# Regrouping the first two chunks of a windowed-attention and feed-forward kernel: tile 0 of the four batches, with exps divided before their transpose

## The chip, the cores and the metric

The kernel runs on one NeuronCore of a Trainium2 chip. The metric is the device time of one execution in microseconds (us). The engines are PE (TensorE, matmuls), DVE (VectorE), ACT (ScalarE), POOL (GpSimd) and SP (SyncE, which issues the DMAs here).

## What is computed

```python
# q, k, v: (4 batches, 8 heads, 768 positions, 64), n_sink = 4, window = 128
scores = q @ k^T / sqrt(64)
keep = (key position < n_sink) | (0 <= row - key < window)
a = softmax(where(keep, scores, -1e9))
x = (a @ v) as (4 * 768 tokens, 512)
h = x @ w_in                      # 512 x 2048
g = where(h > 0, h, exp(min(h, 0)) - 1)
out = g @ w_out                   # 2048 x 512
```

All is float32 to the outside; the weights arrive as 64-bit words.

## The kernel before

Tokens are cut into 24 tiles of 128 (6 for each of the 4 batches, NT = 6), and tiles into chunks. `SIZES` (L42) gives nine chunks of consecutive tiles, 2, 2, 2 and then six of 3. A tile attends to its own and the previous tile of its batch, and to the four sink keys. So tile 0 of a batch has one key block of 4 + 128 columns (KW = 132), every other tile has two (264 columns), and tiles 2 to 5 have the sinks as a separate part. Heads go in four pairs.

For each chunk, attention yields x for four head pairs, each as two float16 parts, high and low. Then the feed-forward runs 16 steps of f (`feed_forward`, L881): 12 matmuls h <- x, w (L902), the exponential unit on ACT and DVE (L910, L912, L915), a split into two float16 parts (L916 on ACT, L918 on DVE in chunk 0 and L921 on POOL elsewhere), and then, two steps later, three matmuls for each tile into accumulators (L932). Chunks 0 and 1 go in halves, (0, first 8 f), (1, first 8 f), (0, last 8 f), (1, last 8 f), because the weights are still arriving: `weights(k)` (L474) loads 32 pieces of 512 KB, rebuilds each value from its 64-bit word (d on ACT L339, sign on DVE L343 or POOL L340, bits on DVE L344, POOL L341 or ACT L342, v on DVE L345) and splits it into two float16 parts (L502 on ACT, L503 on POOL).

There are two attentions. `attention_f32` (L559) serves chunks 0 and 1 (`TURNED`, L50), all in float32: scores (L600), a reduction with the mask (L607, DVE), exps with their sums (L610, ACT), transposes of the exps on PE (L617), their copy out of PSUM (L621), the sums' scaling on POOL (L622) and the reciprocal (L623), sink columns (L628, L643, L646), then values (L658, L663), and a matmul that spreads 1/sum over the partitions (L666). The result is multiplied by 1/sum behind the values: the spread 1/sum goes to SBUF (rx, L679, ACT), DVE multiplies (L680), and the product is split (L682 on ACT, L683 on DVE or POOL). One PSUM bank, `po`, serves all of this in turn. `attention` (L690) serves the other chunks: from chunk 3 on (`WHOLE`) keys and queries are split into float16 parts (L717, L720, L721), scores are two matmuls per head (L791, L792), probabilities are split into two float16 parts (L827, L828), transposed by DMA, and multiplied with both parts of v (L861; sinks L866). Chunk 2 takes its scores in float32 (L797) and the rest as chunks 3 on.

The order of the work comes from a planner (`Plan`, L99): each piece is a task with an engine or a choice of engines, a cost and its dependencies. PE's tasks have hand-given positions (`times`, L518: a slot is half a feed-forward step), the others take due times from their users. Rings (`RINGS`, L53) limit buffers. The masks of tile 1 and of the tiles behind are tasks of their own (L457, L458), as are the limits (L459). In the first 28 us warm-up matmuls (L1273) fill PE's planned pauses. Checks of the value range (L987, L994, L1009) run on DVE with no user but the end.

## Time and profile before

| | |
|---|---|
| time, median of 3 runs | 615.57 us (615.26 to 615.84) |
| time of the profiled execution | 615.47 us |
| its span, first to last instruction | 613.7 us |
| PE busy | 603.9 us (98%), 4608 matmuls |
| DVE busy | 480.3 us (78%) |
| ACT busy | 435.1 us (71%) |
| POOL busy | 263.5 us (43%) |
| granted TensorE clock, mean | 0.998 |

A busy share is an average over stages. In the profile's 40 slices DVE and ACT are at 8 to 9 tenths in the first seven and PE at 9 in all but the first and the last. Line numbers (L902) are those of the kernel before.

### The profile page before, as it was taken

The numbers are of one execution on the slowest core, as the hardware profiler recorded it, in microseconds if no ns is written. First come the engines' busy times: TensorE is split into PE (matmuls) and PEld (weight loads), VectorE is DVE, ScalarE is ACT, GpSimd is POOL, SyncE is SP. The second block draws the span as 40 slices with busy tenths as digits, with TensorE's granted clock in tenths as the row PEclk, the third lists the DMA queues.
The fourth block names the chain that finished last, engine by engine and source line by source line (L and its number), as shares of the span: only waits on it lengthen the run. The fifth ranks groups of instructions, "written<-read, shape, count | busy, mean of one in ns | idle before, by whom it ended". The sixth has DMA issues, their size and how long they took to land.

```text
span 613.7 us, 13669 instructions
## 1 busy us (share of the span) xinstructions
PE 603.9 (98%) x4608; PEld 365.2 (60%) x4608; DVE 480.3 (78%) x1284; ACT 435.1 (71%) x1236; POOL 263.5 (43%) x510
## 2 busy tenths in 40 slices
PE   9899999999999999999999999999999999999996
PEld 6666665677775565655555565655555565555553
DVE  8999989979989877797788988887897987533232
ACT  6999999878888776677677767666876866332222
POOL 3878777543344433333344444223434444222211
PEclk9999999999999999999999999999999999999999
DMA  8776975959789775483867857585756935310001
GB/s 308 266 263 219 239 258 193 232 114 230 193 155 218 160 151 128 105 222 95 180 146 185 210 112 157 129 222 137 199 124 158 232 69 136 98 45 9 2 0 58
DMA packets 117360, 97.54 MB, mean 159 GB/s; under 512 B 88994, under 2 KB 94370, under 8 KB 117282
## 3 DMA queue, kind: packets, MB, share of 16 engines
q1 hardware_dynamic: 117136, 96.53, 61.4%
q8 instruction: 38, 0.62, 0.4%
q14 instruction: 40, 0.33, 0.2%
q10 hardware_dynamic: 146, 0.07, 0.0%
HBM read 67.99 MB, written 7.34 MB: 123 GB/s over the span
## 4 chain that ended last, share of the span: by engine, by line
PE 87%; DVE 6%; ACT 5%; issue 1%; POOL 0%; ACTq 0%; DVEq 0%
PE h L902 37%; PE acc L932 27%; PE last_acc L932 10%; PE s L791 2%; PE s L792 2%; PE last_end L861 2%; PE s L861 2%; ACT last_acc L339 1%; DVE wv L345 1%; DVE e L607 1%; ACT g L910 1%; DVE wu L343 1%; ACT w L502 1%; DVE pt L621 1%; ACT gh L916 1%
## 5 line engine op out<-in xcount | busy, mean ns | idle before, releaser
L902 PE MATMUL h<-x,w 128*128 128x384 f16 (+1 forms) x1728 | 271.9, 308 | 1.0 <-ACT w L502 0.7
L902 PEld LDWEIGHTS <-w 128*128 128x128 f16 x1728 | 167.8, 98 | 88.3 <-issue 1.5
L921 POOL TENSOR_TENSOR gl<-g,gh 128x384 f16<-128x384 f32 (+1 forms) x127 | 113.9, 897 | 177.7 <-ACT gh L916 147.3
L932 PE MATMUL acc<-w,gh 128*128 128x512 f16 x572 | 163.4, 379 | 0.0
L932 PEld LDWEIGHTS <-gh 128*128 128x128 f16 x792 | 74.8, 98 | 69.8 <-ACT g L912 0.7
L910 ACT ACTIVATE g<-h 128x384 f32<-128x384 f32 (+1 forms) x144 | 64.6, 448 | 70.2 <-PE h L902 64.2
L828 DVE SCALAR_TENSOR_TENSOR pq<-e,st,pq 128x256 f16<-128x256 f32 x160 | 86.0, 562 | 17.8 <-ACT pq L827 17.4
L916 ACT ACTIVATE gh<-g 128x384 f16<-128x384 f32 (+1 forms) x127 | 62.2, 490 | 49.4 <-DVE g L915 49.3
L815 ACT ACTIVATE e<-e,st 128x264 f32<-128x264 f32 x160 | 78.3, 490 | 19.8 <-DVE st L813 19.6
L932 PE MATMUL acc<-w,gl 128*128 128x512 f16 x286 | 87.2, 379 | 0.0
L912 DVE TENSOR_SCALAR g<-g 128x384 f32<-128x384 f32 (+1 forms) x97 | 36.7, 378 | 60.2 <-ACT g L910 59.5
L827 ACT ACTIVATE pq<-e,st 128x256 f16<-128x256 f32 x160 | 70.7, 483 | 8.2 <-DVE st L820 3.5
L915 DVE SCALAR_TENSOR_TENSOR g<-g,h 128x384 f32<-128x384 f32 (+1 forms) x128 | 65.9, 515 | 4.3 <-ACT g L912 3.0
L932 PE MATMUL last_acc<-w,gh 128*128 128x512 f16 (+1 forms) x190 | 69.2, 371 | 0.0
L813 DVE CUSTOM_DVE_ANT_0 e<-s,m 128x264 f32<-128x264 f32 x160 | 61.1, 405 | 10.0 <-PE s L792 9.3
L932 PEld LDWEIGHTS <-gl 128*128 128x128 f16 x396 | 38.2, 98 | 44.1
L819 POOL TENSOR_SCALAR st<-st 128x2 f32<-128x2 f32 x80 | 21.6, 270 | 93.4 <-ACT e L815 89.5
L717 ACT ACTIVATE kq<-kqs 128x780 f16<-128x780 f32 (+1 forms) x48 | 42.9, 899 | 10.4 <-PE s L792 8.7
L503 POOL TENSOR_TENSOR w<-wv,w 128x512 f16<-128x512 f32 x32 | 39.3, 1237 | 9.6 <-ACT w L502 7.1
L792 PE MATMUL s<-kq 128*128 128x264 f16 (+1 forms) x144 | 35.4, 267 | 0.0
L791 PE MATMUL s<-kq 128*128 128x264 f16 (+1 forms) x144 | 35.4, 267 | 0.0
L932 PE MATMUL last_acc<-w,gl 128*128 128x512 f16 (+1 forms) x95 | 35.2, 371 | 0.0
(163 smaller groups left out, 825.1 us busy)
## 6 DMA issues: line engine op xcount, KB each, us to landing
raw<-in_wt_dram SPq DMA_DIRECT2D x32, 512.0 KB, 5.1
kqs<-in_kq_dram SPq DMA_DIRECT2D x24, 456.0 KB, 3.7
kqs<-in_kq_dram SPq DMA_DIRECT2D x24, 390.0 KB, 3.3
qk<-in_kq_dram SPq DMA_DIRECT2D x48, 195.0 KB, 4.7
out_dram<-wv SPq DMA_DIRECT2D x21, 256.0 KB, 4.1
vs<-in_vx_dram SPq DMA_DIRECT2D x20, 256.0 KB, 3.2
vm<-in_vx_dram SPq DMA_DIRECT2D x6, 768.0 KB, 6.0
vs<-in_vx_dram SPq DMA_DIRECT2D x12, 320.0 KB, 3.8
```

Of the source, the lines that this page charges most:

```text
L791: nc.tensor.matmul(sp[:, :wd], q, hi[:, c0 : c0 + wd], start=True, stop=False)
L792: nc.tensor.matmul(sp[:, :wd], q, lo[:, c0 : c0 + wd], start=False, stop=True)
L813: red = add("DVE", 0.08 + 0.00104 * wd, lambda ee=ee, me=me, sp=sps[e], m=m, wd=wd: nc.vector.tensor_tensor_reduce(ee, sp[:, :wd], m[:, :w ...
L815: ex = add("ACT", act_us(wd, sums=True), lambda ee=ee, me=me, rs=rs[:, e : e + 1]: nc.scalar.activation(ee, ee, AF.Exp, bias=me, scale=-1. ...
L827: a = add("ACT", act_us(nb * P, True), lambda src=src, hi=hi, re=re: nc.scalar.activation(hi, src, AF.Copy, scale=re), deps=[rr])
L828: b = add("DVE", dve_us(nb * P) + 0.03, lambda src=src, hi=hi, lo=lo, re=re: nc.vector.scalar_tensor_tensor(lo, src, re, hi, ALU.mult, ALU ...
L902: nc.tensor.matmul(hp[:, :n], win[:, part, d, :], xx[:, :n], start=k == 0, stop=k == 3 * ND - 1)
L910: a = add("ACT", act_us(n) + 0.06, lambda gf=gf, hp=hp, sums=sums: nc.scalar.activation(gf, hp[:, :n], AF.Exp, scale=1.0 / G_SCALE, accum_ ...
L915: b = add("DVE", dve_us(n) - 0.035, lambda gf=gf, gd=gd, hp=hp: nc.vector.scalar_tensor_tensor(gd, gf, 0.0, hp[:, :n], ALU.min, ALU.max), ...
L916: th = add("ACT", act_us(n) - (0.03 if near else 0.0), lambda gd=gd, gh=gh: nc.scalar.activation(gh[:, :n], gd, AF.Copy), deps=[b])
L921: tl = add("POOL", pool_us(n), lambda gl=gl, gd=gd, gh=gh: nc.gpsimd.tensor_tensor(gl[:, :n], gd, gh[:, :n], ALU.subtract), deps=[th])
L932: nc.tensor.matmul(to[:, : cols.stop - cols.start], gg[:, i * P : (i + 1) * P], wout[:, part, cols], start=f == f0 and k == 0, stop=f == f ...
```

## The change

The first two chunks become tile 0 of batches 0 and 1, and tile 0 of batches 2 and 3. All other tiles follow batch by batch in chunks of tiles (1, 2) and (3, 4, 5). There are ten chunks: 2, 2, 2, 3, 2, 3, 2, 3, 2, 3. `attention_f32` then meets only tiles with one key block: its sink parts go. The exps are multiplied by 1/sum in place (DVE, or POOL as a choice) ahead of the transpose, which now waits for that; the matmul that spreads 1/sum, the copy rx and the multiply behind the values go, and x's parts are split straight from PSUM. The bank `po` has two halves, po0 and po1, which chunk 0's pairs use in turn. The mask of tile 1 and the limits wait for the last reduction of chunk 0. The output rows of a tile are addressed one by one, since a chunk's tiles need not be consecutive.

```diff
-SIZES = (2, 2, 2, 3, 3, 3, 3, 3, 3)
+CHUNKS = [[0, NT], [2 * NT, 3 * NT], *[[b * NT + t for t in ts] for b in range(B) for ts in ((1, 2), (3, 4, 5))]]
+SIZES = [len(c) for c in CHUNKS]
...
-    sqs = rows("sq", [P, SIZES[1] * P], F32)
-    for t in sqs:
-        nc.gpsimd.memset(t, 0.0)
...
-            po = po_ps[slot("po")]
+            half = 0 if c else p % 2
+            po = po_ps[0][:, half * qc : (half + 1) * qc]
...
-                sc = add("PE", 0.65 if c else 0.6 if nb == 1 else 1.0, scores, mode="rows", deps=[ldk, *freed] if c and k < 1 else [ldk], pos=at[k])
+                sc = add("PE", 0.35 if c or k > 2 else 0.6, scores, mode="rows", deps=[ldk, *freed] if c and k < 1 else [ldk], pos=at[k])
...
-                tr = add("PE", (0.22 if c else 0.26) * nb, turned, deps=exps, pos=at[k] + 1.5)
...
                 rr = add("DVE", 0.1, lambda rs=rs: nc.vector.reciprocal(rs, rs), deps=[rr])
+                even = []
+                for e in range(2):
+                    keys, re = e3[:, e, NS:KW], rs[:, e : e + 1]
+                    even.append(add("DVE", 0.07 + 0.00053 * P, lambda keys=keys, re=re: nc.vector.tensor_scalar(keys, keys, re, None, ALU.mult), deps=[rr], port=True, or_=[("POOL", 0.3, lambda keys=keys, re=re: nc.gpsimd.tensor_scalar(keys, keys, re, None, ALU.mult))]))
...
+                tr = add("PE", 0.22 if c else 0.26, turned, deps=even, pos=at[k] + 1.5)
...
-                    for e in range(2):
-                        nc.tensor.matmul(po[e * D : (e + 1) * D, oc], rs[:, e : e + 1].to_broadcast([P, D]), ident, start=False, stop=end)
...
-            a = add("ACT", act_us(qc) - 0.03, lambda rx=rx, xf=xf: nc.scalar.activation(rx, xf, AF.Copy), deps=[val])
-            b = add("DVE", dve_us(qc) - 0.03, lambda rx=rx, po=po: nc.vector.tensor_tensor(rx, po[:, :qc], rx, ALU.mult), deps=[a])
-            fa = add("ACT", act_us(qc), lambda xh=xh, rx=rx: nc.scalar.activation(xh, rx, AF.Copy), deps=[b])
-            fb = add("DVE", dve_us(qc), lambda xh=xh, xl=xl, rx=rx: nc.vector.tensor_tensor(xl, rx, xh, ALU.subtract), deps=[fa], port=True, or_=[("POOL", ...)])
+            fa = add("ACT", act_us(qc) - 0.03, lambda xh=xh, po=po: nc.scalar.activation(xh, po, AF.Copy), deps=[val])
+            fb = add("DVE", dve_us(qc) - 0.03, lambda xh=xh, xl=xl, po=po: nc.vector.tensor_tensor(xl, po, xh, ALU.subtract), deps=[fa])
+            ring(f"po{half}", [val], [fa, fb])
...
+                if c == 0:
+                    for t in (mask1_, limits_):
+                        t.deps.append(freed[-1])
```

## Rows read from the trace of the kernel before

**Rows 1.** Stretches: length, each engine's busy us (instructions), granted clock, DMA share, GB/s
```profile
25.00:64.40 39.40, 38.44 (x338) 26.08 (x337) 38.42 (x97) 37.15 (x104) 30.96 (x47) 1.00 0.71 242
64.40:81.00 16.60, 16.60 (x126) 12.02 (x125) 14.91 (x36) 16.00 (x49) 14.13 (x25) 1.00 0.95 236
81.00:112.00 31.00, 30.01 (x242) 18.95 (x241) 27.91 (x67) 29.86 (x81) 21.73 (x30) 1.00 0.62 218
112.00:133.00 21.00, 21.00 (x194) 14.74 (x192) 17.86 (x54) 17.70 (x58) 9.87 (x22) 1.00 0.69 165
133.00:187.00 54.00, 54.00 (x489) 37.73 (x484) 49.39 (x148) 46.04 (x145) 21.59 (x52) 1.00 0.88 193
```
The engines stand in the order PE, PEld (weight loads), DVE, ACT, POOL.

**Rows 2.** PE's waits, 20 to 190 us, longest first: total, times, longest
```profile
PE s L1273 <- DVE st L607: 0.9, 1, 0.9
PE h L902 <- ACT w L502: 0.7, 1, 0.7
```

**Rows 3.** PE in order of time: start us, modelled length us
```profile
25.02 1.48 PE L902 MATMUL h<-x,w 128*128 128x256 f16 x12
...
135.89 1.47 PE L902 MATMUL h<-x,w 128*128 128x256 f16 x12
```

**Rows 4.** Chain that ended last: start, length without overlap; float32 attention of chunk 1
```profile
48.02 0.22 PE last_end L643 x2
...
49.55 0.59 PE last_end L658 x8
...
50.58 0.44 PE last_end L658 x8
...
51.45 0.65 PE s L797 x4
...
53.50 0.44 PE last_end L617 x4
```

**Rows 5.** The same chain: float16 attention, scores and values
```profile
119.89 0.06 PE s L791
...
124.02 0.11 PE s L791
...
131.95 0.34 PE last_end L861 x12
132.29 0.06 PE last_end L866 x2
```

**Rows 6.** The same chain: feed-forward halves at two tiles and at three
```profile
111.95 1.29 PE acc L932 x6
...
118.58 1.31 PE h L902 x12
...
192.37 1.95 PE h L902 x12
```

**Rows 7.** DVE, groups by line: shape, count, busy us, mean ns, idle before
```profile
L607 DVE CUSTOM_DVE_ANT_0 e<-s,m 128x264 f32<-128x264 f32 x16 | 6.2, 419 | 0.0
L680 DVE TENSOR_TENSOR rx<-last_end,rx 128x256 f32<-128x256 f32 x8 | 3.3, 413 | 0.6 <-ACT rx L679 0.5
L607 DVE CUSTOM_DVE_ANT_0 e<-s,m 128x132 f32<-128x132 f32 x8 | 2.0, 289 | 0.1
L372 DVE TENSOR_SCALAR m<-sv 128x128 bf16<-128x128 f32 x5 | 1.0, 222 | 0.0
```

**Rows 8.** ACT, groups by line
```profile
L610 ACT ACTIVATE e<-e,st 128x264 f32<-128x264 f32 x24 | 12.1, 505 | 0.3 <-POOL st L622 0.3
L610 ACT ACTIVATE e<-e,st 128x132 f32<-128x132 f32 x8 | 3.1, 391 | 2.7 <-DVE st L607 2.7
L679 ACT ACTIVATE rx<-last_end 128x256 f32<-128x256 f32 x8 | 2.9, 368 | 0.0
```

**Rows 9.** DVE and POOL in order of time around 40 us
```profile
39.03 0.46 DVE L344 TENSOR_SCALAR wu<-raw 128x512 uint16<-128x512 uint16 x1
39.96 2.46 POOL L503 TENSOR_TENSOR w<-wv,w 128x512 f16<-128x512 f32 x2
40.02 1.41 DVE L344 TENSOR_SCALAR wu<-raw 128x512 uint16<-128x512 uint16 x1 [0.16 <-POOL wu L340]
```

More of the change, by code (lines that the diff above doesn't have):

```diff
@@ L565, in attention_f32 @@
         kc, qc = nk * KW, nt * P
-        far = any(g % NT >= 2 for g in ts)
-        kw, vw = kc + qc, (nk + far) * P
+        assert all(g % NT == 0 for g in ts)
+        kw, vw = kc + qc, nk * P
         n = NP * nt
@@ new lines, in turned @@
+                def turned(e3=e3, tp=tp):
+                    for e in range(2):
+                        nc.tensor.transpose(tp[:, e * P : (e + 1) * P], e3[:, e, NS:KW], ident)
+                tr = add("PE", 0.22 if c else 0.26, turned, deps=even, pos=at[k] + 1.5)
+                n = 2 * P
+                cp = add("ACT", act_us(n) - 0.03, lambda tp=tp, pt=pt, n=n: nc.scalar.activation(pt, tp[:, :n], AF.Copy), deps=[tr], or_=[("DVE", dve_us(n) - 0.03, lambda tp=tp, pt=pt, n=n: nc.vector.tensor_copy(pt, tp[:, :n]))])
@@ L635, in attention_f32 @@
                 ring("kqs", [ldk or scored[0]], scored)
-            sk_ = sq = None
-            if far:
-                sq = sqs[slot("sq")]
-                sp = sq[0 : 2 * NS, :]
-                def sinks(po=po, prods=prods):
-                    for v in prods:
-                        nc.tensor.transpose(po[0 : 2 * NS, v[6] * P : (v[6] + 1) * P], v[8][:, 4 : 4 + 2 * NS], ident)
-                sk_ = add("PE", 0.22, sinks, mode="few", deps=[u for v in prods for u in (v[0], v[9])], pos=at[k - 1] + 2.5)
-                cs = add("ACT", act_us(qc) - 0.03, lambda sp=sp, po=po: nc.scalar.activation(sp, po[0 : 2 * NS, :qc], AF.Copy), deps=[sk_], or_=[("DVE", dve_us(qc) - 0.03, lambda sp=sp, po=po: nc.vector.tensor_copy(sp, po[0 : 2 * NS, :qc]))])
-                ring("po", [sk_], [cs])
-                sk_ = cs
@@ L665, in values @@
                     for e in range(2):
-                        nc.tensor.matmul(po[e * D : (e + 1) * D, oc], rs[:, e : e + 1].to_broadcast([P, D]), ident, start=False, stop=end)
-            val = add("PE", 0.03 + 0.216 * sum(v[7] + 1 + far for v in prods), values, mode="columns", deps=[ldv, sk_, *[u for v in prods for u in v[:2]]], pos=at[k - 1] + 4.0)
-            for cp, _, red, *_ in prods:
+                        vo = j * P + e * D
+                        nc.tensor.matmul(po[e * D : (e + 1) * D, j * P : (j + 1) * P], vr[:, vo : vo + D], pt[:, e * P : (e + 1) * P], start=j == 0, stop=j == nt - 1)
@@ L670, in attention_f32 @@
+            val = add("PE", 0.03 + 0.216 * nt, values, mode="columns", deps=[ldv, *[v[0] for v in prods]], pos=at[k - 1] + 4.0)
+            for cp, *_ in prods:
                 ring("pt", [cp], [val])
-                ring("st", red, [val])
-            if far:
-                ring("sq", [sk_], [val])
             if held:
                 ring("vs", [ldv or val], [val])
-            rx = rxs[slot("rx")]
             xh, xl = x_room(qc)
-            xf = po[:, qc : 2 * qc]
-            a = add("ACT", act_us(qc) - 0.03, lambda rx=rx, xf=xf: nc.scalar.activation(rx, xf, AF.Copy), deps=[val])
@@ L741, in taken_values @@
             else:
-                ring("po", [val], [fa, fb])
+                for half in range(2):
+                    ring(f"po{half}", [val], [fa, fb])
                 po_users[:] = [fa, fb]
@@ L1002, in fast_path @@
         kts = key_tiles(CHUNKS[c])
-        a = kts.index(CHUNKS[c][0]) * KW if c > WHOLE else 0
+        a = kts.index(CHUNKS[c][0])
+        a = a * KW if all(any(g in ch for ch in CHUNKS[WHOLE:]) for g in kts[:a]) else 0
         n = KQ_OFF[c, 1] - KQ_OFF[c, 0] - a
```

70 lines of the change are left out of this document (18 added, 52 removed).

## The prediction

> **What bounds the kernel now.** I read the view by stretches first [rows 1]. From 25 us to 187 us TensorE (PE) is busy almost without a break, but the reader should look at the columns beside it: from 25 to 64.4 VectorE (DVE) is busy 38.42 of 39.40 us and ScalarE (ACT) 37.15, from 81 to 112 ACT 29.86 of 31, from 112 to 187 PE all of the time with DVE at 17.86 of 21 and 49.39 of 54. So the opening is held by three engines at once, and PE only after it. Second, who waited for whom on PE [rows 2]: the longest waits after 20 us are 0.9 and 0.7 us, so idle PE is nowhere a large sum. Third, PE in order of time [rows 3]: the first feed-forward matmul starts at 25.02 us, the first one of chunk 2 (after the 32 half-and-half steps of chunks 0 and 1) at 135.89. Fourth, the chain that ended last gives the length of each PE piece without overlap [rows 4 to 6].
>
> The end can therefore be written as: the time at which chunk 2's feed-forward starts (now 135.9), plus the PE work behind it, plus PE's waits. I work out the change of each. The profiled execution took 615.47 us with a span of 613.7, so 1.8 us lie around the span; it is 0.1 us under the median of the runs (615.57), and I add the 1.8 to a span at the end.
>
> **Part 1: PE work behind 135.9 us.** Feed-forward work stays: 24 tiles of 16 steps. A step's second half costs six 512-column matmuls for two tiles, 1.29 us, whatever the chunk; its first half costs 1.31 us at two tiles and 1.95 at three [rows 6]. Two three-tile chunks become three two-tile chunks, 16 x (3 x 1.31 - 2 x 1.95) = +0.5 us, which is at the rounding of the rows; I take 0.4 and keep 0 to 0.5.
> Attention in f16: a tile 0 reads one key block, scores 4 x 0.06 = 0.23 us and values 6 matmuls, half of the 0.34 for 12, so 0.40 per head pair. A tile 1 costs 4 x 0.11 + 0.34 = 0.79, a later tile 0.06 more for its sinks, 0.85 [rows 5]. With four pairs, a chunk of tiles 0, 1, 2 is 8.2 us, one of 3, 4, 5 is 10.2, one of 1, 2 is 6.6. Before there are three of the first and three of the second, 55.2 us. After there are three of the third kind behind chunk 2 and four of the second, 60.6: +5.4, because three cheap tiles 0 leave the f16 path and three dear tiles (3, 4, 5 of batch 0) enter it. One more chunk changes PE's mode a few times more, 0.3 us (bounds 0 and 0.6). Chunk 2 itself stays in f32 scores, with tiles 1, 2 for 4, 5: one sink tile less, -0.2 us, before 135.9. Sum of part 1: +0.4 + 5.4 + 0.3 = +6.1 us.
>
> **Part 2: the opening, up to 135.9 us.** On PE: a pair of chunk 1 now costs two scores at 0.65, two pairs of transposes at 0.44, the sink transposes at 0.22 and values from 49.55 to 51.45, 1.90: 4.3 us, 17.2 for four, of which four scores and one transpose (3.0 us) lie before 25.02 [rows 4]. After, scores have 132 columns for 264 (taken as half, 0.33; bounds 0.33 and 0.65), transposes two of 128 for four (0.22), values four matmuls for the 8 that take 0.44 (0.22), no broadcast of 1/sum through PE and no sinks, one mode change of about 0.1: 1.4 us a pair, 5.8 for four. PE is freed of 14.2 - 5.8 = 8.4 us behind its first step, and 0.2 of chunk 2.
> The first step itself: chunk 0 becomes two one-block tiles as well, the output bank is split in two halves so that pairs alternate, and two mask blocks and the limits move off DVE to behind chunk 0's last reduction. I take 2.5 us earlier (bounds 0 and 5). What is not shortened: the weights of step 0 and the multiply that now stands between exps and transposes. By PE alone chunk 2 would start 8.4 + 0.2 + 2.5 = 11.1 us earlier.
> But PE is not alone. ACT: 24 of 32 exps in the two chunks fall from 0.505 to 0.391 us (2.7), eight copies L679 at 0.368 go (2.9), five wide copies shrink (1.1, estimated at the same slope per column), a sink copy and slightly shorter x copies (0.4 + 0.3): 7.4 us less [rows 8]. DVE: 24 reductions fall from 0.419 to 0.289 (3.1), eight multiplies L680 at 0.41 go (3.3), seven wide copies shrink (1.8, by that slope), three sink copies go (1.2). Added are 32 multiplies of 128 x 128 in SBUF; the nearest row is the 128 x 128 mask operation L372, 0.222 us, 7.0 in all, and x's second half now comes from PSUM, so those that GpSimd (POOL) did go to DVE (0 to 3.3, taken 1.6). DVE is left with 0.8 us less [rows 7].
> These multiplies have the form for which DVE can be held up: the same L344 took 0.46 us at 39.03 and 1.41 at 40.02, while POOL ran two L503 from 39.96 [rows 9]. Bounds of one added multiply: 0.14 (estimated at two thirds of L372, since one begins before the last has ended) and 0.22 + 0.95; the plan may order other work first, or give it to POOL, so I take 0.22 and put the hold-up into a rival.
> The Trainium skill (SBUF — State Buffer, "Who interferes with whom") says that a DVE tensor_scalar in a two-port mode and a GpSimd instruction exclude one another for a whole instruction. The two L344 rows agree. By that rule alone, were every one of chunk 1's 16 multiplies to land beside POOL, DVE would lose up to 15 us and the opening would gain nothing; that is rival A, whose price below goes by the rows.
> What remains is to set 11.1 (PE) against ACT's 7.4 and DVE's 0.8. ACT and DVE share work: copies and the step L912 can go to either, sign and bit steps of the weights to POOL too. The sum 8.2 is 4.1 each. And chunk 2's attention, of which part now runs from 25 to 64.4, can move into the idle time behind: DVE has 1.7, 3.1 and 3.1 us idle in the three stretches from 64.4 to 133, ACT 0.6, 1.1 and 3.3 [rows 1]. So the engines allow from 0.8 (DVE alone, no idle time used) to 4.1 + 5.0 = 9.1 us. I take 8.0, near the upper end, because PE, which fixed the pace from 112 to 133, is what becomes free. Conversions of weights hide PE's freed work only if they are early enough; without that cover the freed PE time becomes a wait and costs what rival A says.
>
> **Part 3: waits behind 135.9.** Now a three-tile attention runs beside two-tile chunks (16 steps of 2.60 us each) four times. The nearest row is the stretch 133 to 187: chunk 2's two-tile steps with a three-tile attention, DVE 49.39 of 54, and PE busy all 54 us [rows 1]. The checks of values and keys, which nothing waits for until the end, can give way. I take 0.4 us in all (bounds 0 and 4). The last chunk has three tiles as before, so the tail stays. The added wait of transposes for the multiply has values and the next tile's scores of the same chunk queued behind it on PE; two chunks only.
>
> Sum: -8.0 + 6.1 + 0.4 = -1.5. Span 612.2, time 614.0 us.
>
> **Rivals.** *A, the conversions keep the opening (slower).* PE's free time from 25 to 64.4 turns into waits for w (L502, L503) and for DVE. For it: DVE is busy 97% there and saves nearly nothing by itself, and its multiplies can be blocked. Against it: POOL is idle 8.4 of 39.4 us and can take steps. Price: the gain is 0.8 + 1.7 = 2.5 us, so -2.5 + 6.1 + 0.4 = +4.0, 619.5 us. It decides against the change once the opening gains less than 5.3 us.
> *B, PE alone sets the opening.* If the plan refits everything, the gain is the PE sum: -11.1 + 6.1 + 0.4 = -4.6, 610.9 us. Against it stands DVE at 97%.
> *C, the dense windows wait.* Four windows with 1 us of PE wait each: -8.0 + 6.1 + 4.0 = +2.1, 617.6 us. Against it: the stretch 133 to 187 has no such wait.
> *D, the reordering does not reach the first step.* If x of chunk 0 arrives no earlier than 25 us because the multiply, POOL's sum and the reciprocal lengthen the chain by what the removed copies shorten, the gain is some 5.5 at the rate of the shared engines: +1.0, 616.5 us.
>
> **How the numbers follow.** Forecast (opening gains 6.5 to 9.5; 612.5 to 615.5 us) 0.43; A 0.20; B 0.17; C 0.08; D 0.12. About 0.2% (1.2 us) is what a measurement can tell from no change. Faster: B and six tenths of the forecast, 0.43. Same: the rest of the forecast (0.17) and most of D (0.10), with 0.01 of C: 0.28. Slower: A, most of C and the end of D, 0.29. Both signs hold much of the chance: the likeliest case's own range is 612.5 to 615.5, and the range to 8 in 10 goes from B (610.7) to just under A's price (619.0).
>
> **What would show it.** In the changed profile: the first h matmul at 22 to 23 us; chunk 2's first h at about 128; no L643, L663, L666 pieces; score pieces of 0.33 us; ACT's exps at 0.39 us; the multiplies at 0.2 us where POOL is idle. PE's waits from 25 to 64 us should be a few us in all. From there the span should hold 484 us to the end for 478 now. Wrong would be the forecast if PE waits for w more than 6 us in the opening, if the multiplies average over 0.5 us, if a 50 us stretch behind 190 us has more than 1 us of PE idle, or if the granted clock falls from the 1.00 of [rows 1] in the longer gaps of the opening.

## The result and the profile after

The changed kernel takes 621.77 us (median of 8 runs, 619.32 to 624.79), the kernel before on the same chip 615.77 (8 runs, 615.07 to 616.46). The ratio is 1.0096, with a 95% interval of 1.0080 to 1.0113: slower by 6.0 us, where the prediction was 614.0 and its range ended at 619.0.

The profiled execution of the changed kernel took 624.12 us with a span of 622.0, so it is one of its longer ones, 2.35 above the median. I keep that in mind below: of its 8.3 us of span over the kernel before (613.7), 6 are typical.

In the changed kernel scores are L592, the reduction L599, exps L602, POOL's step on the sums L605, the reciprocal L606, the new multiplies L610, transposes L615, their copy L619, values L631, x's parts L639 and L640, h L859, and warm-up matmuls L1235.

First PE in order of time: the first matmul of the feed-forward, and the first of chunk 2.

```profile
32.47 1.47 PE L859 MATMUL h<-x,w 128*128 128x256 f16 x12
...
138.85 1.47 PE L859 MATMUL h<-x,w 128*128 128x256 f16 x12
```

Before they stood at 25.02 and 135.89 [rows 3]; 22 to 23 and about 128 were forecast. So the first step comes 7.5 us later instead of 2.5 earlier, and chunk 2 starts 3.0 later instead of 8.0 earlier. From there to the end the changed kernel needs 622.0 - 138.85 = 483.15 us, 5.35 more than before (613.7 - 135.89 = 477.8); 6.5 more were forecast. The whole miss lies in the opening. The view by stretches (columns as in [rows 1]) says of what kind it is; the first fence is the opening of the kernel before, in one stretch,

```profile
0.77:135.89 135.12, 130.91 (x1089) 87.42 (x1090) 123.23 (x358) 122.72 (x359) 90.82 (x160) 1.00 0.74 235
```

and the second the same of the changed kernel, followed by three short stretches of its start and by the part behind the opening:

```profile
0.77:138.85 138.08, 127.44 (x940) 84.58 (x941) 118.25 (x365) 121.04 (x358) 91.25 (x150) 0.98 0.71 226
...
24.00:26.00 2.00, 0.05 (x2) 0.07 (x1) 1.97 (x9) 1.78 (x6) 1.50 (x3) 0.78 0.89 309
26.00:28.00 2.00, 0.85 (x5) 0.61 (x5) 1.77 (x6) 0.59 (x3) 0.81 (x2) 0.50 0.11 45
28.00:30.00 2.00, 2.00 (x11) 1.40 (x9) 0.00 (x0) 0.00 (x0) 0.65 (x1) 0.50 0.00 0
...
187.00:259.70 72.70, 72.70 (x514) 40.96 (x509) 52.14 (x132) 48.68 (x131) 28.06 (x52) 1.00 0.56 139
259.70:330.00 70.30, 70.30 (x607) 47.28 (x605) 66.80 (x185) 56.12 (x167) 31.77 (x72) 1.00 0.88 201
```

In the opening PE's busy time fell only by 3.5 us (130.9 to 127.4) and its idle time rose by 6.4 (135.12 - 130.91 = 4.2 to 138.08 - 127.44 = 10.6); together that is the 3.0 us. DVE and ACT, which were to lose 0.8 and 7.4 us, lost 5.0 and 1.7: the planner gave 11 of the multiplies to POOL, and ACT took 13 bit steps of the weights for 9. Behind 187 us PE has no idle time at all, not even where DVE is busy 66.8 of 70.3 us.

What PE waited for between 3 and 64 us, longest first (total us, times, longest):

```profile
PE s L1235 <- DVE st L599: 3.4, 2, 3.1
PE h L859 <- DVE gl L875: 1.4, 3, 0.7
PE h L615 <- DVE e L610: 1.1, 1, 1.1
PE last_end L631 <- DVE pt L619: 1.0, 1, 1.0
PE s L592 <- DVE st L599: 1.0, 1, 1.0
PE s L592 <- DMA kqs<-in_kq_dram: 0.9, 1, 0.9
```

All but the last are for DVE. Around the longest, in order of time, DVE and then POOL:

```profile
24.14 0.76 DVE L371 TENSOR_SCALAR m<-sv 128x4 bf16<-128x4 f32 x2
24.82 0.15 DVE L606 RECIPROCAL st<-st 128x2 f32<-128x2 f32 x1
24.89 0.40 DVE L640 TENSOR_TENSOR x<-last_end,x 128x256 f16<-128x256 f32 x1
...
25.42 1.47 DVE L610 TENSOR_SCALAR e<-e,st 128x128 f32<-128x128 f32 x2
26.81 0.28 DVE L599 CUSTOM_DVE_ANT_0 e<-s,m 128x132 f32<-128x132 f32 x1
...
25.46 1.15 POOL L498 TENSOR_TENSOR w<-wv,w 128x512 f16<-128x512 f32 x1 [0.38 <-ACT w L497]
```

and PE there, with its start:

```profile
5.86 0.81 PE L592 MATMUL s<-kqs 64*128 64x132 f32 x4 [0.92 <-DMA kqs<-in_kq_dram]
...
13.55 0.81 PE L592 MATMUL acc<-vm 64*128 64x132 f32 x4
...
23.55 0.50 PE L592 MATMUL s<-kqs 64*128 64x132 f32 x4
27.15 2.64 PE L1235 MATMUL s<-const-bfloat16-1.0 128*128 128x248 bf16 x12 [3.11 <-DVE st L599]
...
30.15 0.81 PE L592 MATMUL s<-kqs 64*128 64x132 f32 x4
```

Two multiplies beside POOL's L498 take 1.47 us, the first of them alone 1.27; the reduction behind them starts at 26.81, PE stands for 3.1 us, and in that wait the granted clock falls to 0.50, the lower of its two levels (1.2 of 2.4 GHz): the same score piece takes 0.81 us at 30.15 for 0.50 at 23.55. It also takes 0.81 up to 13.55, where the clock column reads 1.00; the trace has no record of the level before 18.3 us, so that PE is at the lower level there is argued from this length. The twelve warm-up matmuls at 27.15 were planned at 0.11 us each and take 2.64 for all. They are no help in the wait: they write the score bank that the late reduction still reads, and so wait for it themselves.

Last, the multiplies, by engine (shape, count, busy us, mean ns):

```profile
L610 DVE TENSOR_SCALAR e<-e,st 128x128 f32<-128x128 f32 x21 | 7.3, 379 | 0.1
L610 POOL TENSOR_SCALAR e<-e,st 128x128 f32<-128x128 f32 x11 | 7.0, 644 | 4.2 <-DVE st L606 4.1
```

14.3 us for 32, where the sum had 7.0, by 0.222 from [rows 7]. The shortest, median and longest of those on DVE (ns):

```profile
L610 DVE TENSOR_SCALAR e<-e,st x21: 273/283/1270, 7.3 to 49.3; 128x128 f32<-128x128 f32 x21
```

Taken one by one, the 11 with no POOL operation beside them took 0.27 to 0.29 us, the ten with one 0.49 on average. So 0.222 was too low even for an undisturbed multiply.

### The profile page after: what moved, and what is told of

It reads as the page before. It is cut to its first block, busy times and chain, and to the rows that moved or that the text cites. A ratio compares the mean times of both kernels' runs of the same rounds, so it can differ in the third digit from the quotient of the medians.

```text
span 622.0 us, 14215 instructions
## 1 busy us (share of the span) xinstructions
PE 606.3 (97%) x4747; PEld 385.3 (62%) x4747; DVE 486.3 (78%) x1342; ACT 452.6 (73%) x1312; POOL 279.3 (45%) x550
## 4 chain that ended last, share of the span: by engine, by line
PE 83%; ACT 8%; DVE 6%; issue 1%; DMA 1%; SPq 0%; DVEq 0%; ACTq 0%
PE h L859 35%; PE acc L889 29%; PE last_acc L889 6%; PE s L749 3%; PE s L750 3%; PE last_end L819 2%; PE s L819 2%; ACT w L497 2%; ACT last_acc L338 1%; ACT g L867 1%; DVE wv L344 1%; PE s L1235 1%; ACT gh L873 1%; ACT e L773 1%; ACT wu L341 1%
## 5 line engine op out<-in xcount | busy, mean ns | idle before, releaser
L859 PE MATMUL h<-x,w 128*128 128x256 f16 (+1 forms) x1920 | 275.0, 294 | 2.1 <-DVE gl L875 2.0
L859 PEld LDWEIGHTS <-w 128*128 128x128 f16 x1920 | 187.2, 98 | 75.6 <-issue 1.9
L878 POOL TENSOR_TENSOR gl<-g,gh 128x256 f16<-128x256 f32 (+1 forms) x143 | 118.7, 830 | 181.9 <-ACT gh L873 141.6
L867 ACT ACTIVATE g<-h 128x256 f32<-128x256 f32 (+1 forms) x160 | 67.1, 419 | 62.6 <-PE h L859 58.5
L873 ACT ACTIVATE gh<-g 128x256 f16<-128x256 f32 (+1 forms) x143 | 65.6, 459 | 47.5 <-DVE g L872 46.2
L773 ACT ACTIVATE e<-e,st 128x264 f32<-128x264 f32 x160 | 81.2, 508 | 22.4 <-DVE st L771 21.4
L869 DVE TENSOR_SCALAR g<-g 128x256 f32<-128x256 f32 (+1 forms) x101 | 36.9, 366 | 71.4 <-ACT g L867 70.6
L872 DVE SCALAR_TENSOR_TENSOR g<-g,h 128x256 f32<-128x256 f32 (+1 forms) x144 | 68.2, 474 | 5.5 <-ACT g L869 3.7
L674 ACT ACTIVATE kq<-kqs 128x912 f16<-128x912 f32 (+1 forms) x56 | 47.7, 859 | 5.6 <-PE s L750 4.8
L889 PE MATMUL last_acc<-w,gh 128*128 128x512 f16 (+1 forms) x126 | 45.3, 366 | 0.0
L498 POOL TENSOR_TENSOR w<-wv,w 128x512 f16<-128x512 f32 x32 | 38.5, 1208 | 8.4 <-ACT w L497 7.6
L677 DVE SCALAR_TENSOR_TENSOR kq<-kqs,kq 128x528 f16<-128x528 f32 (+1 forms) x56 | 38.6, 690 | 2.0 <-ACT kq L674 1.2
L749 PE MATMUL s<-kq 128*128 128x264 f16 x144 | 37.3, 276 | 0.0
L750 PE MATMUL s<-kq 128*128 128x264 f16 x144 | 37.2, 276 | 0.0
```

Source lines behind the costliest of these rows:

```text
L749: nc.tensor.matmul(sp[:, :wd], q, hi[:, c0 : c0 + wd], start=True, stop=False)
L750: nc.tensor.matmul(sp[:, :wd], q, lo[:, c0 : c0 + wd], start=False, stop=True)
L773: ex = add("ACT", act_us(wd, sums=True), lambda ee=ee, me=me, rs=rs[:, e : e + 1]: nc.scalar.activation(ee, ee, AF.Exp, bias=me, scale=-1. ...
L859: nc.tensor.matmul(hp[:, :n], win[:, part, d, :], xx[:, :n], start=k == 0, stop=k == 3 * ND - 1)
L867: a = add("ACT", act_us(n) + 0.06, lambda gf=gf, hp=hp, sums=sums: nc.scalar.activation(gf, hp[:, :n], AF.Exp, scale=1.0 / G_SCALE, accum_ ...
L872: b = add("DVE", dve_us(n) - 0.035, lambda gf=gf, gd=gd, hp=hp: nc.vector.scalar_tensor_tensor(gd, gf, 0.0, hp[:, :n], ALU.min, ALU.max), ...
```

## The experiments

All numbers in one table. "Behind" is the span less the start of chunk 2; "idle" is PE's idle time from 0.77 us to that start; times are medians, and each ratio is to the kernel before on the same chip (medians of 615.58 to 616.51 there). The first rows are the kernel before and the changed one.

| kernel | first step | chunk 2 | behind | idle | time us | ratio to before |
|---|---|---|---|---|---|---|
| before | 25.0 | 135.9 | 477.8 | 4.2 | 615.77 | |
| after | 32.5 | 138.85 | 483.15 | 10.6 | 621.77 | 1.0096 [1.0080, 1.0113] |
| e9 before, other order | 26.2 | 136.7 | 477.7 | 4.3 | 616.14 | 1.0005 [0.9994, 1.0016] |
| e11 after, other order | 26.0 | 134.4 | 483.3 | 10.5 | 619.64 | 1.0059 [1.0041, 1.0077] |
| e4 regroup only | 24.5 | 130.4 | 483.1 | 5.5 | 617.04 | 1.0019 [1.0008, 1.0031] |
| e12 regroup only, other order | 24.3 | 130.2 | 483.1 | 4.7 | 616.89 | 1.0011 [0.9996, 1.0027] |
| e5 multiply first only | 26.9 | 136.3 | 479.3 | 5.9 | 617.59 | 1.0038 [1.0025, 1.0050] |
| e1 no fillers | 27.6 | 138.0 | 483.2 | 11.7 | 622.67 | 1.0102 [1.0084, 1.0119] |
| e2 gap filled | 27.2 | 133.5 | 483.0 | 9.3 | 620.33 | 1.0087 [1.0063, 1.0111] |
| e6 masks back | 25.3 | 134.2 | 485.2 | 9.8 | 621.25 | 1.0079 [1.0062, 1.0095] |
| e7 masks back, gap filled | 26.1 | 135.0 | 485.3 | 9.8 | 622.54 | 1.0105 [1.0089, 1.0122] |
| e8 e7 with multiplies on ACT | 25.7 | 136.2 | 484.1 | 10.6 | 621.67 | 1.0086 [1.0069, 1.0103] |
| e10 no multiplies | 22.0 | 128.8 | 483.9 | 5.8 | 614.79 | 0.9984 [0.9971, 0.9997] |
| e13 multiplies aside | 22.4 | 136.4 | 483.0 | 10.7 | 621.71 | 1.0089 [1.0073, 1.0106] |
| e14 no POOL step | 24.3 | 131.9 | 484.5 | 7.7 | 618.87 | 1.0046 [1.0029, 1.0063] |
| e17 multiplies on DVE | 25.1 | 134.2 | 485.1 | 7.4 | 620.79 | 1.0086 [1.0064, 1.0108] |
| e18 one multiply per tile | 26.35 | 133.4 | 484.0 | 8.8 | 618.99 | 1.0056 [1.0037, 1.0075] |
| e19 e14 and e18 | 27.7 | 138.6 | 483.5 | 11.0 | 622.09 | 1.0103 [1.0085, 1.0120] |
| e15 before, no POOL step | 28.6 | 139.0 | 477.6 | 4.6 | 617.15 | 1.0021 [1.0011, 1.0031] |
| e16 regroup, no POOL step | 24.45 | 133.3 | 483.1 | 5.1 | 616.26 | 1.0009 [0.9999, 1.0019] |

Every edit makes the planner list the work in another order, so a single number carries the accident of an order with it; the runs with other random numbers say how much.

### Is it the change or its order?

The planner's `random.Random(0)` becomes `random.Random(1)`, in the kernel before (e9) and in the changed one (e11).

> The kernel before with one thing changed: its planner's random numbers start from 1 instead of 0, so that it lists the same work in another order out of its search. It says how much of a difference of a per cent is the change and how much the accident of an order. If orders of one kernel lie within 1 us of each other (614.8 to 616.8 us), the 6 us between before and after are the change's own. If this order is 3 us or more away from 615.8, most of the verdict on the change would be the order's.

> The changed kernel whose planner starts from random number 1 instead of 0, and so finds another order for the same work. If the loss is the change's own, it stays: 620 to 622.5 us, with a first step anywhere from 25 to 32 us and chunk 2's first step at 134 us or later. If the low clock level of the changed kernel's start was an accident of its one order and was the whole loss, an order without it gives chunk 2's first step at 128 to 131 us and 613 to 616 us.

The two orders of the kernel before lie 0.4 us apart, those of the changed one 2.1. The other order of the changed kernel starts its steps at 26.0 instead of 32.5 us and chunk 2 at 134.4 instead of 138.85, and still takes 619.64 us. So the loss is the change's own, some 4 us of it in either order, and up to 2 us more hang on the order that it happened to get.

### The two halves of the change

e4: the new grouping, with attention and scaling as before.

```diff
-SIZES = (2, 2, 2, 3, 3, 3, 3, 3, 3)
+CHUNKS = [[0, NT], [2 * NT, 3 * NT], *[[b * NT + t for t in ts] for b in range(B) for ts in ((1, 2), (3, 4, 5))]]
```

> The new grouping of tiles with the old attention of the first two chunks (1/sum spread by PE behind the values, x divided in SBUF; the masks are not moved). Theory 1 (PE's level and fillers, from too little PE work at the start): again a late first step, 27 to 33 us, time 618 to 624. Theory 2 (multiplies and masks): the first step at 21 to 25 us as planned, time 612 to 617. Behind chunk 2's start all theories expect 483 to 485 us to the end, as in the changed kernel (483.2), for 477.8 before.

e12 is the same in another order.

> The new grouping with the attention and the scaling of the kernel before, in another random order. If the balance of the grouping alone (5.5 us gained up to chunk 2, 5.3 us of TensorE work more behind it) is the grouping's own, chunk 2's first step is again at 129.5 to 131.5 us, 483 us follow, and the time is 616 to 618 us. If the gain up to chunk 2 hung on one order, chunk 2's first step is at 133 us or later and the time 619 us or more.

e5: the old grouping, with the multiply ahead of the transposes and x split from PSUM.

```diff
+                    even.append(add("DVE", 0.07 + 0.00053 * wd, lambda keys=keys, re=re: nc.vector.tensor_scalar(keys, keys, re, None, ALU.mult), deps=[rr], port=True, or_=[("POOL", 0.2 + 0.0008 * wd, lambda keys=keys, re=re: nc.gpsimd.tensor_scalar(keys, keys, re, None, ALU.mult))]))
...
-                tr = add("PE", (0.22 if c else 0.26) * nb, turned, deps=exps, pos=at[k] + 1.5)
+                tr = add("PE", (0.22 if c else 0.26) * nb, turned, deps=even, pos=at[k] + 1.5)
```

> The old grouping with the other half of the change: exps (264 columns, sinks with them) multiplied by 1/sum ahead of their transpose, x split straight from PSUM, one bank without halves. Theory 1: PE loses only the spreading of 1/sum (about 5 us of matmuls in the opening), it stays busy enough, the first step at 24 to 27 us, time 613 to 617. Theory 2: DVE has 64 to 32 more multiplies of up to 264 columns that POOL can block, the first step at 28 us or later, time 618 to 623.

The grouping alone gains 5.5 us up to chunk 2 and pays 5.3 behind it, in both orders. It is the other half that takes the gain back: these two, without it, start chunk 2 at 130.3 us, the changed one in its better order at 134.4. PE's idle time says the same, 5 us without it and 10 with it. On the old grouping, where a multiply has up to 264 columns, that half costs about 2 us. It holds more than the multiplies (x split from PSUM, two halves of the bank, masks moved); e10 below takes them out by themselves.

### The start at the lower clock level

e1 leaves out the warm-up matmuls behind the first nine. e2 puts four more into the pause at 4.9 us (0.92 us, for keys by DMA). e6 lets the mask of tile 1 and the limits run where they ran before (they wait for chunk 0's last reduction in the changed kernel, not chunk 1's as the expectation says), and e7 is e6 with the pause filled too.

```diff
-EARLY, WARM_UNTIL = 9, 28.0
+EARLY, WARM_UNTIL = 9, 0.1
...
-        b.fn = filled(b.fn, first["warm"], s_ps[1] if a.start > 7.0 else h_ps[1], int((b.start - a.start - a.dur - 0.2) / 0.11))
+        b.fn = filled(b.fn, first["warm"], s_ps[1] if a.start > 7.0 else h_ps[1], int((b.start - a.start - a.dur - 0.2) / 0.11) + (4 if a is pe[1] else 0))
...
-                if c == 0:
-                    for t in (mask1_, limits_):
-                        t.deps.append(freed[-1])
```

> The changed kernel without the warm-up matmuls that fill PE's planned pauses in the first 28 us (the nine at the very start stay); the output is the same. In the changed kernel the first feed-forward matmul starts at 32.5 us and 44 such fillers stand in PE's order, 5.7 us of them on the chain that ended last. Theory 1a (the fillers stand in the way: planned at 0.11 us, they take 0.22): without them the first step starts at 26 to 28 us and the time is 616 to 619 us. Theory 1b (PE runs at its lower level at the start, and fewer matmuls keep it there longer): the first step stays at 31 us or later, f32 score pieces stay at 0.8 us beyond 18 us, time 620 to 625. Theory 2 (DVE is what is late: its multiplies blocked by POOL, and the masks that were moved): no change by more than 1 us, the first step at 31 to 33.

> The changed kernel with four more warm-up matmuls ahead of its third score piece, in the 0.9 us that PE waits there for a DMA (4.94 to 5.86 us). Theory 1b (that pause keeps PE at the lower level until 18 us, where the kernel before is at the higher one from 8 us): score pieces of 0.50 us from about 8 us on instead of 18, the first step 3 to 5 us earlier, time 616 to 619 us. Theories 1a and 2: no gain, 0 to 0.9 us later, 621 to 623.

> The changed kernel, but the second mask and the limits have no wait on chunk 1's last reduction, as in the kernel before. Theory 1 (the opening is lost to TensorE's lower clock level, which has two sources: the 0.9 us pause ahead of the third score piece, and the 3 us wait that the moved mask operations help to cause near 24 us): the second source goes, the first stays, so score pieces are still at 0.81 us until some 13 us, the first step falls from 32.5 to 27 to 29 us, chunk 2's first step from 138.9 to 134 to 137, and the time to 617 to 620 us. Theory 2 (the multiplies ahead of the transposes are what holds the opening, the masks only fill VectorE's idle time elsewhere): first step 31 to 33 us, time 621 to 622 us.

> The changed kernel with the mask operations where they were and four more warm-up matmuls ahead of the third score piece. Theory 1 (both sources of the lower clock level are gone): score pieces 0.50 us from about 8.5 us on, no wait of 3 us near 22 us, first step at 22 to 25 us, chunk 2's first step at 128 to 132 us, and with 483 us behind that a span of 611 to 615 and a time of 613 to 617 us. Theory 2 (the multiplies hold the opening): waits of 1 to 3 us on the multiplies or the reductions between 14 and 27 us remain, first step 27 us or later, chunk 2's first step 133.5 as with the gap filled alone, time 619 to 621 us.

Without the warm-up matmuls the first step comes at 27.6 us, but at the lower level, by the length of its twelve matmuls (2.77 us instead of 1.47), and the time is 622.67: nothing won. With the pause filled, score pieces take 0.50 us from 8.6 us on; a wait of 3.0 us for DVE's reduction remains at 22.5, and the median is 620.33, whose interval overlaps that of the changed kernel. In e6 and e7 both the early pieces and the stretch around 25 us run at the higher level. PE in order of time in e6, a score piece and the first step:

```profile
8.23 0.50 PE L592 MATMUL s<-vm 64*128 64x132 f32 x4
...
21.09 1.35 PE L1232 MATMUL s<-const-bfloat16-1.0 128*128 128x248 bf16 x11 [1.28 <-DVE st L599]
...
25.27 1.47 PE L859 MATMUL h<-x,w 128*128 128x256 f16 x12
```

The first step stands at 25.27, no earlier than before. The theory that the lower level is the whole loss falls here: 621.25 and 622.54 us, not 613 to 617. The fall of the clock goes with the late first step of the changed kernel's profiled execution, but orders without the fall leave the opening 6 us short of the forecast. (In the profiled execution of e6 6.3 us lie behind the last matmul, for 4.2 in the changed kernel; this is where e6, e7 and e17 have 2 us more behind chunk 2, and it has nothing to do with the opening. Why is not known.) e7 shows one thing by the way. In its order, which is that of e6, the pause was planned full, so the four extra matmuls only delay PE by 0.85 us; the first step, chunk 2 and the end all come 0.8 to 0.9 us later.

### The multiplies

e10: e6 without the 32 multiplies; the transposes wait for the exps alone.

```diff
-                    even.append(add("DVE", 0.07 + 0.00053 * P, lambda keys=keys, re=re: nc.vector.tensor_scalar(keys, keys, re, None, ALU.mult), deps=[rr], port=True, or_=[("POOL", 0.3, lambda keys=keys, re=re: nc.gpsimd.tensor_scalar(keys, keys, re, None, ALU.mult))]))
...
-                tr = add("PE", 0.22 if c else 0.26, turned, deps=even, pos=at[k] + 1.5)
+                tr = add("PE", 0.22 if c else 0.26, turned, deps=exps, pos=at[k] + 1.5)
```

> The changed kernel with the mask operations where they were and with the 32 multiplies by 1/sum left out (the transposes wait for the exps alone; the exps of chunks 0 and 1 are not divided by their sums). Theory 1 (before the first step no engine is the bound: the chain score, reduction, exp, 1/sum, multiply, transpose, copy runs through VectorE, ScalarE and GpSimd, and the multiplies, 0.39 us on VectorE and 0.64 us on GpSimd instead of 0.22, stand in it): first step 22 to 23.5 us instead of 25.3, chunk 2's first step at 129 to 131 us instead of 134.2, time 614 to 617 us. Theory 2 (TensorE's share and the order of the weight conversions decide, the multiplies are hidden): first step 24.5 us or later, chunk 2's at 133 us or later, time 619.5 to 621.5 us.

This is the run that decides. First step 22.04, chunk 2 at 128.8, 614.79 us: all three what the prediction said of the changed kernel (22.5, about 128, 614.0). Against e6 the 32 multiplies cost 5.4 us at chunk 2 and 6.5 us in the end; of the 6.5, 1.7 lie behind the last matmul (6.3 us in e6, 4.6 here), so 5.4 is the figure for the opening. It is one order of each, where two orders of the changed kernel lie 2.1 us apart. The stretch up to chunk 2, e6 and then e10:

```profile
0.77:134.20 133.43, 123.68 (x952) 81.82 (x953) 118.64 (x361) 119.01 (x358) 92.25 (x151) 1.00 0.75 235
```

```profile
0.77:128.80 128.03, 122.25 (x932) 80.52 (x933) 111.94 (x354) 115.78 (x346) 83.05 (x139) 0.99 0.78 243
```

DVE, ACT and POOL are busy 329.9 us in the first and 310.8 in the second, 19.1 more; the multiplies themselves are 16.2 (in e6, 18 on DVE at 0.393 and 14 on POOL at 0.699). PE's own busy time differs by 1.4 us only, and its idle time by 4.

e13 asks whether they cost by standing in the chain or by their work: all 32 run, but write a tile that nothing reads.

```diff
+    idle_out = [pool.tile([P, P], F32, name=f"idle_out{i}") for i in range(2)]
...
-                    even.append(add("DVE", 0.07 + 0.00053 * P, lambda keys=keys, re=re: nc.vector.tensor_scalar(keys, keys, re, None, ALU.mult), deps=[rr], port=True, or_=[("POOL", 0.3, lambda keys=keys, re=re: nc.gpsimd.tensor_scalar(keys, keys, re, None, ALU.mult))]))
+                    even.append(add("DVE", 0.07 + 0.00053 * P, lambda keys=keys, re=re: nc.vector.tensor_scalar(idle_out[0], keys, re, None, ALU.mult), deps=[rr], port=True, or_=[("POOL", 0.3, lambda keys=keys, re=re: nc.gpsimd.tensor_scalar(idle_out[1], keys, re, None, ALU.mult))]))
...
-                tr = add("PE", 0.22 if c else 0.26, turned, deps=even, pos=at[k] + 1.5)
+                tr = add("PE", 0.22 if c else 0.26, turned, deps=exps, pos=at[k] + 1.5)
```

> As the changed kernel with masks back, and all 32 multiplies still run, but they write a tile that nothing reads, and the transposes wait for the exps alone (so the exps of chunks 0 and 1 stay undivided). The engines carry the same work; only its place in the chain score, exp, 1/sum, multiply, transpose is gone. If the multiplies cost by standing in the chain: first step 22 to 23 us, chunk 2's first step 129 to 131 us, time 615 to 617 us, near the kernel without multiplies (22.0, 128.8, 614.8). If they cost by filling VectorE and GpSimd and the port between them: first step 24.5 us or later, chunk 2's at 133 us or later, time 619 to 621.5 us, near the kernel with masks back (25.3, 134.2, 621.3).

Both, at different places. The first step is at 22.42, as without them: before it the chain counts. But the second step comes only at 28.3 (25.3 in e10) and chunk 2 at 136.4, and the time is 621.71: behind it the work counts. The multiplies also hold the buffers of the exps here, but the trace shows one wait of 0.2 us for that. PE's two largest waits up to chunk 2 in e13, and the largest in e10:

```profile
PE h L860 <- POOL w L499: 3.3, 4, 1.6
PE s L1233 <- DVE st L600: 3.0, 3, 1.5
```

```profile
PE h L859 <- ACT w L497: 1.6, 1, 1.6
PE s L1232 <- DVE st L599: 1.3, 3, 0.7
PE h L859 <- POOL w L498: 0.8, 1, 0.8
```

With the weights from ACT (0.2 us in e13), waits for weights are 3.5 us for 2.4 in e10, those for reductions 3.0 for 1.3; together they are 2.8 of the 4.9 us by which PE's idle time is longer, and the rest is spread. POOL did 19 of the 32 multiplies in this order, 12.8 us in which it converted no weights.

```profile
L611 POOL TENSOR_SCALAR idle_out<-e,st 128x128 f32<-128x128 f32 x19 | 12.8, 675 | 3.4 <-DVE st L607 2.6
```

Does it matter where the multiplies run? e8 (as e7) puts all on ACT, e17 (as e6) all on DVE; the two lines take the place of the one with the choice.

```diff
+                    even.append(add("ACT", act_us(P), lambda keys=keys, re=re: nc.scalar.activation(keys, keys, AF.Copy, scale=re), deps=[rr]))
...
+                    even.append(add("DVE", 0.07 + 0.00053 * P, lambda keys=keys, re=re: nc.vector.tensor_scalar(keys, keys, re, None, ALU.mult), deps=[rr], port=True))
```

> As the kernel with masks back and gap filled, but all 32 multiplies by 1/sum run on ScalarE, away from the port that VectorE and GpSimd share. Theory 1 (the clock level and the masks were the loss, the multiplies cost what the sum said): ScalarE gains 32 x 0.3 = about 10 us of work in the opening, where it was the fullest engine after TensorE, so the first step is 1 to 3 us later than with the multiplies on VectorE and GpSimd and the time 1 to 3 us longer. Theory 2 (multiplies of 0.5 to 1.4 us on VectorE, held by the port, are the loss): the reductions are no longer late, first step 2 us or more earlier, and the time 2 us or more shorter than that of the kernel with masks back and gap filled.

> The changed kernel with masks back, all 32 multiplies on VectorE, none on GpSimd: the form that the prediction priced at 32 x 0.222 = 7.1 us. If the loss came from GpSimd's slow multiplies (14 of 0.70 us, 9.7 us that keep it from the weights): VectorE's multiplies go to 0.22 to 0.30 us, the time falls to 617 to 619 us. If VectorE's work itself is what the opening waits for: 620 to 622 us, with multiplies still near 0.39 us where GpSimd's weight steps run beside them.

On ACT they take 0.39 us, and ACT is busy 125.4 us of the opening for 119.1 in e7; 621.67 for 622.54 us. On DVE they take 0.32, and DVE is busy 122.8 us for 118.6 in e6; 620.79 for 621.25. Whichever of the engines gets them, the time stays within a microsecond. e8 was to be 1 to 3 us slower than e7 or 2 us or more faster, and is 0.9 faster: neither. Why the place doesn't matter is argued: all three engines convert weights and serve the exponential unit. The largest sum of PE's waits up to chunk 2 in e6 and e17 is that for gl, the low part that DVE makes behind that unit, 4.6 and 3.0 us (1.7 in e8); for weights the trace lists none in e6, 0.9 in e17 and 1.6 in e8. The line is of e6:

```profile
PE h L859 <- DVE gl L875: 4.6, 5, 2.0
```

So cheaper forms should help. e14 (as e6) takes POOL's step between the sum and its reciprocal away and applies the scale in the multiply; e18 (as e6) makes one multiply of two; e19 does both.

```diff
-                rr = add("POOL", 0.26, lambda rs=rs: nc.gpsimd.tensor_scalar(rs, rs, 1.0 / X_SCALE, 1.0e-9 / X_SCALE, ALU.mult, ALU.add), deps=exps, port=False)
-                rr = add("DVE", 0.1, lambda rs=rs: nc.vector.reciprocal(rs, rs), deps=[rr])
+                rr = add("DVE", 0.1, lambda rs=rs: nc.vector.reciprocal(rs, rs), deps=exps)
...
+                keys, re = e3[:, :, NS:KW], rs[:, :, None].to_broadcast([P, 2, P])
+                even.append(add("DVE", 0.42, lambda keys=keys, re=re: nc.vector.tensor_tensor(keys, keys, re, ALU.mult), deps=[rr], port=True))
```

> As the changed kernel with masks back, without GpSimd's step between the sum and its reciprocal (16 operations of 0.21 us and a hand-over each): VectorE takes 1/sum of the sum as it is, and the multiply applies the scale as its second operand. The multiplies stay. If each step of the chain counts: the first step comes 0.5 to 2 us earlier (23.3 to 24.8 us) and the time is 1 to 3 us shorter (618 to 620 us). If only the engines' work counts: VectorE's is the same, so the first step is at 25 us or later and the time 620.5 to 621.5 us.

> As the kernel with masks back, but one multiply of 128 x 256 with the two reciprocals broadcast, on VectorE, in place of two of 128 x 128: 16 operations of 0.41 us by the rows of the same form and size (the split of x, 0.41), 6.6 us in place of 6.9 on VectorE plus 9.7 on GpSimd. If the engines' work sets the opening: 1 to 3 us shorter than with masks back, 618 to 620 us. If not: 620.5 to 622 us.

> Both cheaper forms at once: one multiply per tile, and no GpSimd step between sum and reciprocal (the scale is the multiply's own constant). Of this chain only the reciprocal and one multiply are left, 16 x (0.16 + 0.41) = 9.1 us on VectorE and nothing on GpSimd. If the multiplies' work and place are the whole of the loss beside the grouping's 5.3 us behind chunk 2: between the 618.9 us without the GpSimd step and the 614.8 us without multiplies, 615 to 618 us, and the first step at 22.5 to 24.5 us. If some other part of the opening holds: 619 us or more.

e14 and e18 are 2.4 and 2.3 us under e6 by the medians, on three different chips, and 2.0 and 1.4 us by the ratios, whose intervals overlap with that of e6. That is what was expected if work and chain count, but no more than two orders of the changed kernel differ. (The wide multiply took 0.544 us on average, not 0.41: the two with no POOL operation beside them 0.41 to 0.42, the other 14 0.56 on average and up to 0.895.) e19 should have gained most and is no better than the changed kernel. PE in its start, and two stretches of it:

```profile
20.41 1.20 PE L1230 MATMUL s<-const-bfloat16-1.0 128*128 128x248 bf16 x6 [0.84 <-DVE st L599]
...
25.01 2.43 PE L1230 MATMUL s<-const-bfloat16-1.0 128*128 128x248 bf16 x11 [1.60 <-DVE st L599]
...
27.66 2.77 PE L857 MATMUL h<-x,w 128*128 128x256 f16 x12
```

```profile
20.00:21.00 1.00, 0.59 (x5) 0.45 (x5) 0.43 (x4) 1.00 (x6) 0.92 (x2) 0.83 0.67 148
26.00:28.00 2.00, 2.00 (x11) 1.60 (x10) 0.78 (x2) 0.03 (x1) 0.00 (x0) 0.50 0.00 0
```

Its order has five waits of 0.3 to 1.6 us from 13 to 25 us. The granted clock falls to the lower level between 20 and 21 us, behind the fourth (0.84), and the first step takes 2.77 us. That the clock takes back what the cheaper chain saves is not shown: this execution is the slowest of four (624.13 us at a mean clock of 0.991), and the other three, at 0.997, still take 621.6 to 622.5. Why e19 loses stays open.

### Work taken from POOL elsewhere

e15 is the kernel before, e16 the regrouped one of e4, both without POOL's step on the sums (the scale goes into ACT's copy of the spread 1/sum).

> The kernel before without GpSimd's step between the sum and its reciprocal in chunks 0 and 1 (16 operations); ScalarE applies the scale in the copy of the reciprocals out of PSUM, at no instruction more. In the changed kernel the same edit was worth 2.4 us, where the step stood ahead of the transposes. In the kernel before it stands ahead of the product with the values alone, beside transposes and copies. If its worth is the freed GpSimd time (3.4 us, which turns to weights): 613.5 to 615 us. If it is the shorter chain ahead of the transposes: no change, 615.5 to 616.5 us.

> The new grouping with the attention and scaling of the kernel before, without GpSimd's step between the sum and its reciprocal. The grouping alone gave 616.9 to 617.0 us. If freed work on the engines that convert weights is worth its time also here: 614.5 to 616 us, at or under the kernel before. If not: 616.5 to 617.5 us.

No gain: 617.15 us for e15, against 615.58 on the same chip, and 616.26 for e16, 0.7 under e4 and e12. (The profiled executions of both, from which the table has its other columns, are their longest, 618.47 and 618.34 us; e15's starts its first step at 28.6.) So POOL's step brings nothing here, and what e14 won isn't that step's time by itself. It may be the chain ahead of the transposes, POOL's multiplies, which took 0.457 us on average in e14 (17 of them) for 0.699 in e6, or an order; that stays open, as does whether any order of e16 is under the kernel before. No run that computes the whole is faster than the kernel before.

## Why the prediction was wrong

**Part 1, PE work behind chunk 2's start: right.** +6.1 and 0.4 of waits were forecast, +5.35 measured, 5.3 in e4 and e12 and 5.5 in e11. So the sum for the dear tiles of batch 0 in the f16 path, from [rows 5], fits; it was not measured piece by piece. The three-tile half step is again 1.95 us, as in [rows 6]. The waits of rival C didn't come: PE is busy throughout from 138.85 to 544 us.

**Part 2, PE alone: near in size.** PE was to be free for 11.1 us and the gain to be 8.0. Without the multiplies the opening gains 7.1 us, PE's busy time up to chunk 2 is 8.7 us less than before, and the first step comes at 22.0 for 22.5 (e10). That e10 meets the forecast so closely is in part luck: the forecast counted 7.0 us of multiplies, and e10 has none.

**Part 2, the multiplies: here it failed.** The step was "DVE is left with 0.8 us less" and, behind it, "I take 8.0, near the upper end". The term in it that was mis-sized is the 32 multiplies, 7.0 us at the 0.222 of [rows 7]. They took 14.3 us: 0.379 each for 21 on DVE, 0.644 for 11 on POOL. [rows 9] had shown the hold-up, and I bounded one multiply at up to 1.17 us (the longest took 1.27), but then took 0.22, less than any of them took, and moved the hold-up into a rival. The mask operation that gave the price took 0.416 us itself in the changed kernel (five of them). And the 7.0 us on POOL had no place in the sum at all.

The step behind it failed too: from totals of busy time to a gain. DVE and ACT together were to lose 8.2 us in the opening and lost 6.7, so their totals came near; PE still idled 6.4 us longer. A total doesn't say when a result is ready, and what PE waited for were single results, of DVE above all. To make up for the work behind chunk 2 the opening had to gain 5.35 us. Without the multiplies it gains 7.1 (e10), with them 1.7 (e6), with all of them on DVE 1.7 too (e17), and with all on ACT it loses 0.3 (e8). How the 5.4 divides between the chain, POOL's time and the hold-up is not shown.

That multiplies are held up beside POOL is shown by the rows at 25.4 us above: the one that took 1.27 us ends 0.08 us behind POOL's L498, and the undisturbed ones took 0.27 to 0.29. The Trainium skill (SBUF — State Buffer, "Who interferes with whom") says that a tensor_scalar in a two-port mode and a GpSimd instruction exclude one another, and the trace agrees; that these multiplies ran in such a mode no run here shows.

**Part 2, the first step: the wrong engine.** "I take 2.5 us earlier" was argued from removed work, but before the first step the chain of exps, sums, reciprocal, multiply and transpose decides (e10 and e13: 22.0 and 22.4 with the multiplies out of the chain; e6: 25.3 with them in it). The prediction named that multiply as what is not shortened, and then didn't price it. What was left was just rival D's case: no earlier than 25 us.

**The clock: named, not priced.** The prediction listed a fall of the granted clock in the opening's longer gaps as what would make it wrong. It fell to 0.50 in a wait of 3.1 us, and the profiled first step stands at 32.5 us. Where no such fall shows it stands at 26.0 and 25.3 (e11, e6), but in other orders of the work, so the difference isn't the clock's alone. Its share in the median is about 2 us at most, an estimate from the 619.64 of the other order and the 621.25 with the masks back. The other signs that it named did not come, and it was wrong all the same: PE waited for w only 0.3 us, the multiplies averaged 0.47, and no stretch behind 190 us has idle PE before the tail.

**Rival A came nearest.** PE's freed time turned into waits, as A said, but for DVE far more than for weights (0.3 us in the changed kernel), with chunk 2 at 134.4 to 133.4 in e11, e6 and e18, a gain of 1.5 to 2.5 us where A said 2.5, and 619.0 to 621.3 us where A said 619.5. In the changed kernel's own order, in the profiled execution, chunk 2 even comes 3.0 us later than before. Rival B fell at once. What spoke for A in the prediction, DVE busy 97% from 25 to 64 us [rows 1], was the stronger argument; what spoke against it, POOL's idle time, was used, and at 0.64 us for a multiply it was no cheap place.

## What to carry to other kernels

Here TensorE, VectorE and ScalarE were all over 90% busy up to chunk 2, and work moved from TensorE to another engine wasn't hidden. In such a stretch, price the added operations at the duration that the same form shows when it is held up, on each engine that may get them, and only then weigh the freed TensorE time. Don't stop at totals of busy time: read what sets the first step from the chain up to it, not from the work that falls away. And where TensorE's work at the start gets thinner, look for the waits that this opens, since the clock can fall in them, as it did here.

## What the hardware showed that I had not expected

A float32 multiply of 128 x 128 by a value for each partition, in place in SBUF, took 0.27 to 0.29 us on DVE with no POOL operation beside it, 0.32 on average where POOL had none of them (e17), 0.38 to 0.39 where POOL shared them, and 1.27 in the longest case, beside one POOL operation of 1.15 us; on POOL 0.64 to 0.70, on ACT 0.39. One of 128 x 256 on DVE with a broadcast operand from SBUF took 0.41 to 0.42 with no POOL operation beside it (two of e18's 16) and 0.544 on average, where the split of x with one operand in PSUM takes 0.413. The lower clock level came back in the first 30 us in a wait of 3.1 us in the changed kernel and behind one of 0.84 us in e19, and the changed kernel's score pieces of the first 13 us have the length of that level while the clock column reads 1.00, since the trace's records of the level begin at 18.3 us.
